# One routing search prepared in two parts instead of four, and low parts of probabilities moved from VectorE to GpSimd in heads 23 to 29

## The chip, the cores and the metric

The kernel runs on one core of a Trainium2 chip. The metric is the device time of one execution in microseconds. Three timed runs of the kernel before gave 721.38, 722.83 and 725.23 us, median 722.83 us; the profiled execution took 720.61 us.

## The reference

Attention in 4 batches of 8 heads, 768 queries and keys, 64 channels; a query sees only the keys of its own hash bucket. Then a mixture of 8 experts, in which every token goes to one expert and every expert takes 384 tokens, filled in the order of the logits.

```python
q_bits = (np.einsum('bhsd,dk->bhsk', q, proj) > 0)
...
scores = np.where(mask, scale * np.matmul(q, k.transpose(0, 1, 3, 2)), -1e9)
attn = np.exp(scores - np.max(scores, axis=-1, keepdims=True))
attn = attn / (np.sum(attn, axis=-1, keepdims=True) + 1e-09)
x = np.matmul(attn, v)            # then (3072 tokens, 512)
logits = x @ w_gate
for idx in np.argsort(-logits.flatten()):
    tok, e = (int(idx) // E, int(idx) % E)
    if assigned[tok] >= 0 or counts[e] >= cap: continue
    assigned[tok] = e; counts[e] += 1
out[mask] = np.maximum(x[mask] @ w1[e], 0.0) @ w2[e]
```

## The kernel before

**Steps.** Attention goes through 32 heads (head 8b+j belongs to batch b), and each head through 6 steps, one for each chunk of 128 keys; heads 30 and 31 end it. The order of all instructions is written out by hand: `ORD='SF0r1LRA'` says in which order a step issues its parts, and a dictionary `at` holds other work by half step (step t has the half steps 2t, issued at `r`, and 2t+1, issued at `R`), so that 12 half steps are one head. A number n in the change is such a half step: 326 lies in head 27.

**The parts of a step.** `S` is a pass for the row maximum of a later head, nine steps ahead: TensorE makes 768 masked scores for 128 queries into `pss` (L250), which has two buffers, and VectorE reduces them to one column (L252). `0` and `1` make the scores of one chunk of keys in halves of 384 queries (L281, L282) and ScalarE takes the exponential into `pt` (L283). `L` makes the low part of the last step's probabilities: `lo` is `pt` in float32 less its own upper 16 bits (L287 for one chunk, L290 for two at once). Which engine does it is a table: for each head a list of chunks that VectorE takes (a number 10+i means chunks 2i and 2i+1 in one instruction); GpSimd takes the rest. `A` multiplies four steps later the high and low parts with the values (L304 to L306), and after a head's last chunk a small product subtracts what the maximum's row added (L310, L311). VectorE then divides (`norm`, L318 to L322, into `X`).

**Between heads.** Once a head's six reductions are done, TensorE transposes the maxima into a buffer of `pss` (`m_rows`, L261) and ScalarE writes them to a row of `qa` (L262). TensorE takes its instructions in order, so a pass or an `m_rows` whose reduction is late holds all behind it. After each second head ScalarE copies the quotients to float16 (`xhigh`, L330), VectorE subtracts (`xlow`, L332), and a DMA transposes the result; after a batch's last head the logits of the batch are made on TensorE (L361, L362) and summed by VectorE (L363).

**The early search.** The first expert's search needs for each of 24 columns of tokens (6 for each batch) the best expert, a sort key and its first digit. `early` gives ten VectorE instructions for a range of columns: L568 to L573, L581, L577, L578 and the comparison with 128 thresholds, L586. Before the change it is called once for each batch, and its instructions are spread five half steps apart, from half steps 268, 300 and 332 for the first three batches; those of the last batch run after attention, when TensorE has only the search to do. GpSimd also makes, for each group of four heads, four low parts of queries and keys (L139).

```python
def lo(h,kc,eng,n=1):
    ...
    eng.tensor_tensor(l,p,p.bitcast(BF)[:,1::2],op=ALU.subtract)
```

Of the kernel before, what the change touches and what calls it, by code (L numbers as in the profile page):

```python
# [8 lines left out]
F32 = mybir.dt.float32  # L9
# [9 lines left out]
AP=dict(PAT=[[10], [5]],  # L19
 ORD='SF0r1LRA',  # L20
 LAG=4,
 VM=[2, 2, 2, 2],
 LL=[4, 3, 3, 2, 2, 2],
 EL={30: [10, 3, 4, 5], 31: [10, 11, 4, 5]},
 E0=[3, 5],
 E1=[],
 X=[4, 4, 18, 14],
 XE=0,
 MR=2,
 LEAD=9,  # L30
# [5 lines left out]
 P4=[-33, -33, -25, -21, -13, -7, -11, -7, -20, -16, -5, -2, -7, 5, 8, 3, 1, 4, 14, -56, -51, -11],  # L36
 CV=[3, 4, 5, 6],
 L0=[89, 4],
 EA=[268, 32, 5],
 MO=['', 'AKs', 'BqLk', 'lm', 'c|ABqKLslmk', 'ABqKLsklm|c', 'ABqKLsklm|c'],  # L40
 MD=[2, 9, 8],
 MV=[23, 24, 28, 57, 96, 1],
# [7 lines left out]
def attention(tc, nc, ctx, qT, kT, vv, proj, wg, x_dram, L, jp, identf, ident, B, late=None, after=None):  # L50
# [4 lines left out]
    psT=ctx.enter_context(tc.tile_pool(name="psT",bufs=NB["T"],space=PS))  # L55
    psV=ctx.enter_context(tc.tile_pool(name="psV",bufs=NB["V"],space=PS))
# [26 lines left out]
    wps=psV.tile([128,512],F32,name="psv")  # L83
# [208 lines left out]
    def AV(h,kc):  # L292
# [14 lines left out]
        if kc==5:  # L307
            for c in range(6):

                if j==3: T.matmul(av[:,c,:],QA[u][96:128,j,c*128:c*128+128],WF[u][96:128,j,:],start=False,stop=(c==5),skip_group_check=True,tile_position=(96,0))  # L310
                else: T.matmul(av[:,c,:],QA[u][:,j,c*128:c*128+128],WF[u][:,j,:],start=False,stop=(c==5),skip_group_check=True)  # L311
    X={}; XS={}; normed=set(); turned={}
    def norm(h):
        d=h//2
        if h%2==0: X[d]=dp.tile([128,6,128],F32,name="X")
        av=AVt[h][:,0:390].rearrange("p (c d) -> p c d",c=6)
        r=dp.tile([128,6],F32,name="r6")
        V.tensor_scalar(r,av[:,:,64],1e-9,1.0/SX,op0=ALU.add,op1=ALU.mult)  # L318
        V.reciprocal(r,r)
        normed.add(h)  # L320
        for c0,c1 in ((0,3),(3,6)) if h==NH-1 else ((0,6),):
            V.tensor_tensor(X[d][:,c0:c1,h%2*64:h%2*64+64],av[:,c0:c1,0:64],r[:,c0:c1,None].to_broadcast([128,c1-c0,64]),op=ALU.mult)  # L322
    XT6=XT.rearrange("p d c q -> p (d c q)").bitcast(F16).rearrange("p (d c z q) -> p d c z q",d=4,c=6,z=2)
# [3 lines left out]
    def xhigh(g):  # L327
        need(g,0,1)
        XS[g]=dp.tile([128,6,2,128],F16,name="XS")
        A.copy(XS[g][:,:,0],X[g])  # L330
    def xlow(g,eng):
        eng.tensor_tensor(XS[g][:,:,1],X[g],XS[g][:,:,0],op=ALU.subtract)  # L332
        xout(g,True)
    def xpart(g,x,c0=0,c1=6):
        need(g,x)
        if x==0: XS[g]=dp.tile([128,6,2,128],F16,name="XS")
        r=slice(64*x,64*x+64)
        A.copy(XS[g][:,c0:c1,0,r],X[g][:,c0:c1,r])
        V.tensor_tensor(XS[g][:,c0:c1,1,r],X[g][:,c0:c1,r],XS[g][:,c0:c1,0,r],op=ALU.subtract)
    def xout(g,turn):  # L340
        b,d=divmod(g,4)
        if turn: turned[d]=b; SY.dma_start_transpose(XT6[:,d].rearrange("p c z q -> p (c z) q"),XS[g].rearrange("p c z q -> p (c z q)"))
        SY.dma_start(x_dram[b*768:(b+1)*768,256*d:256*d+256].rearrange("(c p) e -> p c e",p=128),XS[g].rearrange("p c z q -> p c (z q)"))
# [23 lines left out]
    def add(n,f,*a):  # L367
        if n>=2*(6*NH+LAG+6): raise ValueError('an operation has no step')
        at.setdefault(n,[]).append((f,a))
# [8 lines left out]
    n=-1; early=[]  # L378
# [6 lines left out]
    for G in range(1,NG):  # L385
# [11 lines left out]
        for j in range(4):  # L397
            n=48*(G-1)+AP['CV'][j] if G>3 else p[15]+st*j
# [10 lines left out]
    for h in range(1,NH,2):  # L409
        b,d=h//8,h%8//2; n=2*(6*h+5+LAG)+AP['X'][0]  # L410
        if h==NH-1: n=2*(6*h+5+AP['LL'][5])
        if h==NH-1:
            for c in (0,3): add(n,xpart,4*b+d,1,c,c+3)
            for hf in range(2): add(n+AP['X'][1]*hf,xtr,b,d,hf)
            add(n+4,logits,b,[d]); add(n-5,xpart,4*b+d,0)
            add(n,xout,4*b+d,False)
        else:
            add(n,xhigh,4*b+d); add(n+AP['X'][1],xlow,4*b+d,(V,G_)[AP['XE']])
        if h==NH-1: pass
        elif b==B-1: add(n+AP['X'][3],logits,b,[d])  # L420
        elif d==3: add(n+AP['X'][2],logits,b,range(4))
        if after and d==3:
            for i,f in enumerate(after(b,lambda: psT.tile([128,512],F32,name="pst"),lambda: psV.tile([128,512],F32,name="psv"))):
                add(n+5 if b==B-1 else max(n+AP['X'][2]+3,AP['EA'][0]+AP['EA'][1]*b)+AP['EA'][2]*i,f)
    for n,f in enumerate(late or ()): add(AP['L0'][0]+AP['L0'][1]*n,f)
    for n in sorted(x for x in at if x<0):
# [10 lines left out]
    def step(o,t):  # L437
# [8 lines left out]
        elif o=='L' and t>=1 and (t-1)//6<NH:  # L446
            hh,ss=divmod(t-1,6)
            on=AP['E0'] if hh<1 else AP['E1'] if hh<2 else AP['EL'].get(hh,AP['PAT'][hh%len(AP['PAT'])])
            if 10+ss//2 in on:
# [38 lines left out]
class Moe:  # L488
    def __init__(s, tc, nc, ctx, N):
        s.tc,s.nc,s.N=tc,nc,N  # L490
        s.NC=NC=N//128; s.CAP=N//8
        s.cp=ctx.enter_context(tc.tile_pool(name="mcp",bufs=1)); s.zp=ctx.enter_context(tc.tile_pool(name="mzp",bufs=2))
        s.IDX={}; s.XG={}; s.W={}; s.WIX={}; s.late=[]; s.pend=[]; s.gate=None

    def consts(s):

        nc,NC,cp=s.nc,s.NC,s.cp; G_=nc.gpsimd; A=nc.scalar
        todo=[]
        def iota(shape,pat,cm=0,base=0,name=None,dt=F32):
            t=cp.tile(shape,dt,name=name)  # L500
            todo.append(lambda: G_.iota(t,pattern=pat,base=base,channel_multiplier=cm,allow_small_or_imprecise_dtypes=True))
            return t
        def fill(shape,v,name,dt=F32):
            t=cp.tile(shape,dt,name=name)
            todo.append(lambda: G_.memset(t,v)); return t
# [4 lines left out]
        todo.append(lambda: G_.tensor_tensor(s.ntri,s.ntri,ntd,op=ALU.add))  # L510
        s.ones=fill([128,128],1.0,"mones",BF); s.one48=fill([128,2*NC],1.0,"one48")
        col=lambda v,n,dt=BF: fill([128,1],v,n,dt).to_broadcast([128,128])
# [18 lines left out]

        s.gp=cp.tile([128,2,2,NC],BF,name="gp")
        for i,v in enumerate((1.0,-1.0)):
            todo.append(lambda i=i,v=v: A.activation(s.gp[:,i,0,:],iof[:,0:NC],AF.Copy,scale=128.0*v))
            todo.append(lambda i=i,v=v: A.activation(s.gp[:,i,1,:],pcol.to_broadcast([128,NC]),AF.Copy,scale=v))
        s.th=iota([128,4,NC],[[128,4],[0,NC]],0,4097,name="th")
# [72 lines left out]

    def z(s,shape,dt,name,**k): return s.zp.tile(shape,dt,name="z"+name,**k)  # L610

    def early(s,b,ps,wps,nb=4):

        NC=s.NC; n=NC//nb; c0=b*n
        if b==0:
            s.Z={k:s.z(sh,dt,k,bufs=1) for k,sh,dt in (
                ("m",[128,NC],F32),("eq",[128,NC,8],F32),("mx",[128,NC],F32),("mxu",[128,NC],BF),("OH",[128,NC,8],BF),
                ("key",[128,NC],I32),("D",[128,6,NC],I32),("E",[128,6,NC],BF))}
            s.Z["cmp"]=[s.z([128,NC//2,32 if i else NT[0],2],BF,f"cmp{i}",bufs=1) for i in range(3)]
        todo=s.best(s.Z,c0,c0+n,True)  # L620
        todo.append(lambda: s.compare(s.Z["cmp"][0],0,s.Z["E"][:,0],c0,c0+n))
        if b==nb-1:
            def rest():
                s.ps0=ps; s.wps=wps; s.ph0=s.phase(0)
                for _ in range(7): next(s.ph0)
            todo.append(rest)
        return todo
# [318 lines left out]
@with_exitstack  # L946
def tile_bucket_attention_moe(ctx, tc, qT, kT, vv, proj, wg, w1, w2, out):
    nc = tc.nc
    B = qT.shape[0] // 2
    drp = ctx.enter_context(tc.tile_pool(name="drp", bufs=1, space=DR))  # L950
    x_dram = drp.tile([768 * B, 1024], F16, name="x_dram")
    M = Moe(tc, nc, ctx, 768 * B)
    late = M.consts()
    with ExitStack() as c1:
        c1.enter_context(tc.manual_schedule())
        attention(tc, nc, c1, qT, kT, vv, proj, wg, x_dram, M.Lm, M.jp, M.identf, M.ident, B, late, M.early)
    with ExitStack() as c2:
        M.open(c2, x_dram, w1, w2, out)
        with tc.manual_schedule():
            M.start()  # L960
            M.run()
# [34 lines left out]
```

## Time and profile before

| what | value |
|---|---|
| median of three timed runs | 722.83 us |
| the profiled execution's own time | 720.61 us |
| its span | 718.8 us |
| TensorE (PE) busy | 662.8 us, 92% |
| VectorE (DVE) busy | 545.0 us, 76% |
| GpSimd (POOL) busy | 527.8 us, 73% |
| ScalarE (ACT) busy | 391.4 us, 54% |

The shares are means over stages that differ. In the 40 slices of the page, of 18 us each, attention fills the first 21 or so; TensorE's granted clock is at full speed there, falls where the first search runs, and is back for the experts. The page's table of groups names the costliest instructions; its chain of waits ends at the last DMA and says nothing of attention. For this change the stretch to look at is the last third of attention.

### The profile page before, as it was taken

Reading aid. Unit: us, or ns where it says so; the run is one execution under the profiler, and the core shown is the slowest. Engines: PE = TensorE matmul, PEld = TensorE weight load, DVE = VectorE, ACT = ScalarE, POOL = GpSimd, SP = SyncE. Lnnn points to the kernel's source line nnn. Section 1 sums busy time; section 2 is a strip of 40 time slices with the busy share of each in tenths; the row PEclk is TensorE's granted clock in tenths of the full one; section 3 lists DMA queues with packets and bytes.
Section 4 is the critical chain, followed back from the end, with each engine's and each line's share of the span. In section 5 each row is a group of like instructions: output and inputs, shape, how many; then the busy total and the mean of one; then the engine's idle time right before and its main releaser. Section 6 shows DMA issues by size and latency. Waiting matters only on the chain. (4 is left out here: it accounts for less than half of the span.)

```text
span 718.8 us, 19139 instructions
## 1 busy us (share of the span) xinstructions
PE 662.8 (92%) x7874; PEld 429.9 (60%) x7889; DVE 545.0 (76%) x1231; ACT 391.4 (54%) x772; POOL 527.8 (73%) x463
## 2 busy tenths in 40 slices
PE   8899998999999999889897679989899999999995
PEld 2466675777767776667675465555555555555552
DVE  6888887889899898999878755787788787834120
ACT  5767775867777777656562142434444444444530
POOL 7598979988888988767630365777778787887851
PEclk8899999999999999999998568999999999999998
DMA  8539858826778376542012352626181717272601
GB/s 220 157 94 197 206 145 205 198 66 150 166 168 201 63 175 135 137 100 47 2 46 68 102 179 73 221 70 238 45 279 58 267 58 265 60 278 97 239 17 45
DMA packets 63520, 99.49 MB, mean 138 GB/s; under 512 B 28116, under 2 KB 54088, under 8 KB 61384
## 3 DMA queue, kind: packets, MB, share of 16 engines
q1 hardware_dynamic: 56568, 52.11, 30.5%
q0 software_dynamic: 6784, 46.14, 18.3%
q8 instruction: 62, 1.02, 0.6%
q14 instruction: 26, 0.21, 0.1%
q10 hardware_dynamic: 80, 0.00, 0.0%
HBM read 59.53 MB, written 12.58 MB: 100 GB/s over the span
## 5 line engine op out<-in xcount | busy, mean ns | idle before, releaser
L287 POOL TENSOR_TENSOR lo<-pt 128x768 f16<-128x768 f32 x137 | 230.5, 1699 | 50.4 <-ACT pt L283 46.8
L283 ACT ACTIVATE pt<-pst 128x384 f32<-128x384 f32 x384 | 171.1, 491 | 94.8 <-PE pst L282 91.9
L252 DVE TENSOR_REDUCE m<-pss 128x1 f16<-128x770 f32 x192 | 180.6, 955 | 32.6 <-PE pss L250 32.0
L306 PE MATMUL psv<-vh,lo 128*128 128x65 f16 x1152 | 124.1, 194 | 3.1 <-POOL lo L287 3.1
L281 PE MATMUL pst<-qa,ka 128*128 128x384 f16 x384 | 125.3, 327 | 1.6 <-ACT qa L267 0.8
L282 PE MATMUL pst<-qb,kb 128*128 128x384 f16 x384 | 125.3, 327 | 1.0 <-DMA qb<-ql 1.0
L304 PE MATMUL psv<-vh,pt 128*128 128x65 f16 x1152 | 124.7, 194 | 0.2 <-DVE X L322 0.2
L305 PE MATMUL psv<-vl,pt 128*128 128x64 f16 x1152 | 124.7, 193 | 0.0
L304 PEld LDWEIGHTS <-pt 128*128 128x128 bf16 x1152 | 107.1, 98 | 17.0 <-issue 3.1
L305 PEld LDWEIGHTS <-pt 128*128 128x128 bf16 x1152 | 105.9, 98 | 10.3
L306 PEld LDWEIGHTS <-lo 128*128 128x128 f16 x1152 | 105.9, 97 | 3.9 <-POOL lo L287 3.7
L250 PE MATMUL pss<-ka,qa 128*128 128x385 f16 x384 | 95.5, 331 | 11.7 <-DVE m L252 8.1
L852 PE MATMUL ph<-xx,wh 128*128 128x384 f16 (+1 forms) x544 | 102.6, 323 | 2.8 <-DVE hl L855 2.8
L829 POOL TENSOR_TENSOR wl<-wf,wh 128x512 bf16<-128x512 f32 x87 | 98.5, 1151 | 0.1
L817 ACT CAST wh<-wf 128x1024 f16<-128x1024 f32 x64 | 65.6, 1043 | 31.1 <-DVE un L757 21.0
L854 ACT ACTIVATE hh<-ph 128x384 f16<-128x384 f32 x64 | 31.4, 490 | 82.2 <-PE ph L852 82.2
L852 PEld LDWEIGHTS <-wh 128*128 128x128 f16 x544 | 51.4, 100 | 34.7 <-issue 5.3
L855 DVE SCALAR_TENSOR_TENSOR hl<-ph,hh 128x384 f16<-128x384 f32 x64 | 34.7, 553 | 34.4 <-ACT hh L854 33.8
L864 PEld LDWEIGHTS <-hh 128*128 128x128 f16 x384 | 34.9, 97 | 34.4
L852 PE MATMUL ph<-xx,wl 128*128 128x384 f16 (+1 forms) x272 | 54.8, 322 | 0.0
L282 PEld LDWEIGHTS <-kb 128*128 128x128 f16 x384 | 37.4, 97 | 23.6 <-issue 3.4
L281 PEld LDWEIGHTS <-ka 128*128 128x128 f16 x384 | 37.6, 98 | 22.8 <-issue 2.3
(266 smaller groups left out, 1198.3 us busy)
## 6 DMA issues: line engine op xcount, KB each, us to landing
vp<-in_vv_dram SPq DMA_DIRECT2D x8, 768.0 KB
x_dram<-XS SPq DMA_DIRECT2D x16, 384.0 KB
qp<-in_qT_dram SPq DMA_DIRECT2D x7, 768.0 KB
kp<-in_kT_dram SPq DMA_DIRECT2D x7, 768.0 KB
qa<-qh SPq DMA_DIRECT2D x14, 192.0 KB
ka<-kh SPq DMA_DIRECT2D x14, 192.0 KB
qb<-qh SPq DMA_DIRECT2D x14, 192.0 KB
kb<-kh SPq DMA_DIRECT2D x14, 192.0 KB
```

Of the source, the lines that this page charges most:

```text
L250: T.matmul(ps[:,hf,0:HK],QA[u][:,j,qc*128:qc*128+128],KA[u][:,j,hf*HK:hf*HK+HK],start=True,stop=True)
L252: V.tensor_reduce(M6[h][:,qc:qc+1],ps[:,:,0:HK],axis=AX.XY,op=ALU.max,negate=True)
L281: T.matmul(ps[:,0:384],KA[u][:,j,kr],QA[u][:,j,r],start=True,stop=False)
L282: T.matmul(ps[:,0:384],KB[u][:,j,kr],QB[u][:,j,r],start=False,stop=True)
L283: A.activation(PT[h,kc][0][:,r],ps[:,0:384],AF.Exp,scale=0.125)
L287: eng.tensor_tensor(l,p,p.bitcast(BF)[:,1::2],op=ALU.subtract)
L304: T.matmul(av[:,c,:],ph[:,r],VH[u][:,j,kc,:],start=(kc==0 and c==0),stop=False,skip_group_check=True)
L305: T.matmul(av[:,c,0:64],ph[:,r],VL[u][:,j,kc,:],start=False,stop=False,skip_group_check=True)
L306: T.matmul(av[:,c,:],l[:,r],VH[u][:,j,kc,:],start=False,stop=False,skip_group_check=True)
L817: s.nc.scalar.copy(h[:,r],f[:,r])
L829: for _ in range(n): s.nc.gpsimd.tensor_tensor(*s.pend.pop(0)[1],op=ALU.subtract)
L852: T.matmul(p[:,r],a[:,o:o+128],b[:,d,r],start=n==0 and not c,stop=n==11 and c in (None,2),skip_group_check=c is not None)
```

## The change

The table `EL` gets lists of its own for heads 23 to 29. Before, even heads had [10] there and odd heads [5], 10 chunks together on VectorE; now 6, and GpSimd makes 4 more. The early search of the first three batches is called once, for 18 columns, in place of three times for 6, with its first instruction at half step 326. The copy to float16 comes half a step later after each pair of heads. The logits of the first three batches come one and a half steps later, and those of the first three pairs of heads of the last batch one step later.

```diff
- EL={30: [10, 3, 4, 5], 31: [10, 11, 4, 5]},
+ EL={23: [], 24: [10], 25: [11], 26: [], 27: [3], 28: [3], 29: [], 30: [10, 3, 4, 5], 31: [10, 11, 4, 5]},
- X=[4, 4, 18, 14],
+ X=[5, 4, 20, 15],
- EA=[268, 32, 5],
+ EA=[262, 32, 5],
+ EG={2: 0, 3: 3},
...
-        if after and d==3:
-            for i,f in enumerate(after(b,...
+        if after and d==3 and b in AP['EG']:
+            for i,f in enumerate(after(AP['EG'][b],b,...
                 add(n+5 if b==B-1 else max(n+AP['X'][2]+3,AP['EA'][0]+AP['EA'][1]*b)+AP['EA'][2]*i,f)
...
-    def early(s,b,ps,wps,nb=4):
-        NC=s.NC; n=NC//nb; c0=b*n
-        if b==0:
+    def early(s,a,b,ps,wps,nb=4):
+        NC=s.NC; c0=a*NC//nb; c1=(b+1)*NC//nb
+        if a==0:
...
-        todo=s.best(s.Z,c0,c0+n,True)
+        todo=s.best(s.Z,c0,c1,True)
```

On VectorE, before the quotients of head 23 (the rows L318 belong to them; `m` are maxima, `lo` low parts, `zeq`, `zkey`, `zmxu` the early search), the order before was:

```order
L571 TENSOR_TENSOR zeq<-zeq,wt 128x48
L252 TENSOR_REDUCE m_5975<-pss 128x1 x3
L572 TENSOR_TENSOR zkey<-zm,zkey 128x6
L287 TENSOR_TENSOR lo<-pt 128x768
L252 TENSOR_REDUCE m_5975<-pss 128x1 x2
L290 TENSOR_TENSOR lo<-pt 128x1536
L573 TENSOR_REDUCE zmxu<-zeq 128x6
L252 TENSOR_REDUCE m_6215<-pss 128x1
L318 TENSOR_SCALAR r_6244<-psv 128x6
```

At the same place the changed kernel has (its line numbers are one higher):

```order
L253 TENSOR_REDUCE m_5972<-pss 128x1 x5
L291 TENSOR_TENSOR lo<-pt 128x1536
L253 TENSOR_REDUCE m_6209<-pss 128x1
L319 TENSOR_SCALAR r_6238<-psv 128x6
L320 RECIPROCAL r_6238<-r_6238 128x6
L323 TENSOR_TENSOR X<-psv,r_6238 128x6x64
```

The single low part and three instructions of the early search are gone; the pair of low parts stays. Between the quotients of heads 27 and 28, VectorE had before:

```order
L570 TENSOR_SCALAR zkey<-zm 128x6
L252 TENSOR_REDUCE m_7171<-pss 128x1
L586 TENSOR_TENSOR zcmp_370<-zE,tb_93 128x768
L252 TENSOR_REDUCE m_7171<-pss 128x1
L571 TENSOR_TENSOR zeq<-zeq,wt 128x48
L252 TENSOR_REDUCE m_7171<-pss 128x1 x2
L332 TENSOR_TENSOR XS<-X,XS 128x6x128
L252 TENSOR_REDUCE m_7171<-pss 128x1
L572 TENSOR_TENSOR zkey<-zm,zkey 128x6
L252 TENSOR_REDUCE m_7392<-pss 128x1
L318 TENSOR_SCALAR r_7422<-psv 128x6
```

and has now:

```order
L253 TENSOR_REDUCE m_7155<-pss 128x1
L288 TENSOR_TENSOR lo<-pt 128x768
L253 TENSOR_REDUCE m_7155<-pss 128x1
L573 TENSOR_TENSOR zkey<-zm,zkey 128x18
L253 TENSOR_REDUCE m_7155<-pss 128x1 x2
L574 TENSOR_REDUCE zmxu<-zeq 128x18
L333 TENSOR_TENSOR XS<-X,XS 128x6x128
L253 TENSOR_REDUCE m_7155<-pss 128x1
L253 TENSOR_REDUCE m_7374<-pss 128x1
L319 TENSOR_SCALAR r_7404<-psv 128x6
```

Four instructions of the early search became two, and head 28's low part of chunk 3 stands here in place of a pair one head boundary earlier. On TensorE at attention's end, the last two logits of the third pair of heads of the last batch (L362, from `XT`) stood before the products of the last head's last chunk (L304):

```order
L362 LDWEIGHTS XT
L362 MATMUL pss<-wgs,XT 128x8
L304 LDWEIGHTS pt
L304 MATMUL psv<-vh_209,pt 128x65
L305 LDWEIGHTS pt
L305 MATMUL psv<-vl_210,pt 128x64
```

Now these logits (L362 and L363 with the new numbers) follow those products and their last correction (L311):

```order
L311 LDWEIGHTS qa_171
L311 MATMUL psv<-wf_212,qa_171 128x65
L362 LDWEIGHTS XT
L362 MATMUL pss<-wgs,XT 128x16
L362 LDWEIGHTS XT
L362 MATMUL pss<-wgs,XT 128x16
```

They moved behind everything that the last head's quotients wait for, and stand in front of the transposes of these quotients. GpSimd's list has 33 low parts where it had 29 after its last low part of keys, with nothing else moved.

## Rows read from the trace of the kernel before

**Rows 1.** Busy time by stretch: us, PE, PEld, DVE, ACT, POOL, clock, DMA.

```profile
200.00:290.00 90.00, 88.69 (x1407) 64.48 (x1399) 79.36 (x102) 65.32 (x146) 78.61 (x58) 1.00 0.67 153
290.00:374.00 84.00, 75.83 (x1208) 56.15 (x1207) 77.21 (x107) 51.11 (x104) 53.78 (x33) 1.00 0.28 65
```

**Rows 2.** The same view of four shorter stretches.

```profile
298.00:304.00 6.00, 3.65 (x56) 2.57 (x53) 5.93 (x9) 3.72 (x8) 2.44 (x2) 1.00 0.47 108
312.00:318.00 6.00, 3.94 (x68) 2.82 (x65) 5.90 (x9) 2.76 (x7) 2.71 (x3) 1.00 0.61 116
336.00:350.00 14.00, 12.23 (x192) 8.80 (x189) 12.84 (x22) 7.54 (x15) 7.97 (x5) 1.00 0.25 59
350.00:364.00 14.00, 12.09 (x182) 8.74 (x182) 10.93 (x15) 8.72 (x18) 10.84 (x7) 1.00 0.24 58
```

**Rows 3.** Waits of PE from 290 to 374: us in total, times, longest.

```profile
PE pss L250 <- DVE m L252: 3.6, 6, 2.0
PE pss L261 <- DVE m L252: 2.8, 2, 1.9
```

**Rows 4.** Timeline at the first two gaps: start, duration, instruction, [idle before].

```profile
295.52 2.29 DVE L287 TENSOR_TENSOR lo<-pt 128x768 f16<-128x768 f32 x1
299.47 2.70 DVE L290 TENSOR_TENSOR lo<-pt 128x1536 f16<-128x1536 f32 x1
303.20 0.49 PE L250 MATMUL pss<-ka,qa 128*128 128x385 f16 x2 [2.05 <-DVE m L252]
313.12 1.42 DVE L577 TENSOR_TENSOR zE<-zD,sc 128x6 bf16<-128x6 int32 x1
```

**Rows 5.** Timeline, PE at an earlier boundary of heads.

```profile
279.48 0.49 PE L250 MATMUL pss<-ka,qa 128*128 128x385 f16 x2 [0.46 <-DVE m L252]
```

**Rows 6.** DVE groups from 255 to 389.2, early search: busy us, mean ns.

```profile
L577 DVE TENSOR_TENSOR zE<-zD,sc 128x6 bf16<-128x6 int32 x3 | 3.4, 1119 | 0.0
...
L573 DVE TENSOR_REDUCE zmxu<-zeq 128x6 bf16<-128x48 f32 x3 | 0.6, 189 | 0.0
```

**Rows 7.** Timeline, DVE: first and last early instruction of the last batch.

```profile
389.30 0.20 DVE L568 TENSOR_REDUCE zm<-Lm 128x6 f32<-128x48 f32 x1
...
390.54 0.56 DVE L586 TENSOR_TENSOR zcmp<-zE,tb 128x768 bf16<-128x768 bf16 x1
```

**Rows 8.** Groups by form: the comparison of 24 columns in later searches.

```profile
L586 DVE TENSOR_TENSOR zcmp<-zE,tb 128x3072 bf16<-128x3072 bf16 x5 | 8.8, 1753 | 0.0
```

**Rows 9.** Timeline, DVE: a pair and a single of low parts.

```profile
346.06 1.75 DVE L290 TENSOR_TENSOR lo<-pt 128x1536 f16<-128x1536 f32 x1
...
366.77 0.95 DVE L287 TENSOR_TENSOR lo<-pt 128x768 f16<-128x768 f32 x1
```

**Rows 10.** GpSimd's low parts from 290 to 374, as a group.

```profile
L287 POOL TENSOR_TENSOR lo<-pt 128x768 f16<-128x768 f32 x31 | 51.3, 1672 | 29.4 <-ACT pt L283 29.3
```

**Rows 11.** Timeline, GpSimd: head 23's chunk 4, and the longest low part.

```profile
295.53 1.46 POOL L287 TENSOR_TENSOR lo<-pt 128x768 f16<-128x768 f32 x1
...
346.47 2.67 POOL L287 TENSOR_TENSOR lo<-pt 128x768 f16<-128x768 f32 x1 [4.73 <-ACT pt L283]
```

**Rows 12.** Timeline, PE: the correction that ends head 23.

```profile
299.71 0.35 PE L310 MATMUL psv<-wf,qa 32*128 32x65 f16 x6
```

**Rows 13.** Timeline, DVE: quotients of heads 25 and 26.

```profile
327.85 0.56 DVE L322 TENSOR_TENSOR X<-psv,r 128x384 f32<-128x384 f32 x1
...
337.72 0.56 DVE L322 TENSOR_TENSOR X<-psv,r 128x384 f32<-128x384 f32 x1
```

**Rows 14.** Timeline, PE at attention's end.

```profile
383.71 0.30 PE L361 MATMUL pss<-wgs,XT 128*128 128x16 f16 x6
...
386.57 0.87 PE L351 MATMUL pst<-identf,X 128*128 128x128 f32 x6 [0.88 <-DVE X L322]
```

**Rows 15.** ScalarE groups from 0 to 390: exponentials and copies of quotients.

```profile
L283 ACT ACTIVATE pt<-pst 128x384 f32<-128x384 f32 x384 | 171.1, 491 | 94.8 <-PE pst L282 91.9 <-POOL ql L139 1.3 <-POOL lo L287 0.2
...
L330 ACT CAST XS<-X 128x768 f16<-128x768 f32 x15 | 12.5, 832 | 0.3
```

More of the change, by code (lines that the diff above doesn't have):

```diff
@@ L421, in attention @@
         elif d==3: add(n+AP['X'][2],logits,b,range(4))
-        if after and d==3:
-            for i,f in enumerate(after(b,lambda: psT.tile([128,512],F32,name="pst"),lambda: psV.tile([128,512],F32,name="psv"))):
+        if after and d==3 and b in AP['EG']:
+            for i,f in enumerate(after(AP['EG'][b],b,lambda: psT.tile([128,512],F32,name="pst"),lambda: psV.tile([128,512],F32,name="psv"))):
                 add(n+5 if b==B-1 else max(n+AP['X'][2]+3,AP['EA'][0]+AP['EA'][1]*b)+AP['EA'][2]*i,f)
@@ L619, in early @@
             s.Z["cmp"]=[s.z([128,NC//2,32 if i else NT[0],2],BF,f"cmp{i}",bufs=1) for i in range(3)]
-        todo=s.best(s.Z,c0,c0+n,True)
-        todo.append(lambda: s.compare(s.Z["cmp"][0],0,s.Z["E"][:,0],c0,c0+n))
+        todo=s.best(s.Z,c0,c1,True)
+        todo.append(lambda: s.compare(s.Z["cmp"][0],0,s.Z["E"][:,0],c0,c1))
         if b==nb-1:
```

## The prediction

> **What bounds the kernel now.** I read the page's slices first: TensorE is the engine nearest to full in attention, and from slice 17 on it is less full than before although its clock stays up. The view of busy time by stretch puts numbers on that [rows 1]. From 200 to 290 us PE is busy 88.69 of 90 us, so it sets the pace; 1.31 us are lost. From 290 to 374 it is busy 75.83 of 84, so 8.17 us are lost, while VectorE is busy 77.21 of 84 and GpSimd only 53.78. The clock is 1.00 in both. Four shorter stretches [rows 2] hold nearly all of the loss: 6.00 - 3.65 = 2.35 us at 298 to 304, 2.06 at 312 to 318, 1.77 at 336 to 350 and 1.91 at 350 to 364, together 8.09. In the first two VectorE is full (5.93 and 5.90 of 6). The waits name the cause [rows 3]: PE waits for row maxima, 3.6 us in front of a pass and 2.8 us in front of the transposes of a head's maxima. The reductions themselves are not slow; the timeline shows what stands in front of them [rows 4]: a low part of 2.29 and a pair of 2.70 us, then a pass of PE that has waited 2.05; later a six-column product of the early search that takes 1.42 us.
>
> So in this third of attention VectorE's list sets the end, at the boundaries of heads, and what it is spared can be worth up to 8.1 us. All that follows attention starts from its end, so what is won there moves the end of the kernel by as much.
>
> **The early search.** Before, the first three batches take thirty VectorE instructions, in ten groups of three that run from 3.4 us down to 0.6 [rows 6], 16.3 us in all. The same ten instructions for the last batch run when GpSimd has nothing, and there they take from 0.20 (the first) to 0.56 us (the comparison), 2.2 us for the ten [rows 7]. Thirty without disturbance would be 6.6 us; 9.7 us are therefore stretching, 0.32 us for each. The ten new ones have three times the columns. The comparison lies between 0.56 us for 6 columns [rows 7] and 1.75 for 24 [rows 8]; on the straight line 18 columns cost 1.35. The other nine are near their fixed cost at 6 columns; I give five of them (48 elements to 144) 0.12 us more each, an estimate that is small beside the rest. Alone: 2.2 + 0.8 + 0.6 = 3.6 us. With the same stretching for each, 10 x 0.32, the sum is 6.8. VectorE is spared 16.3 - 6.8 = 9.5 us, nothing of it in the last batch, whose ten are the same.
>
> **What stretches them.** The product L577 takes 1119 ns on average over the three batches [rows 6] while the whole of the last batch's ten takes 2.2; the reduction L573 keeps its 189 ns. GpSimd's low parts are stretched too: 1672 ns on average, 1.46 for an undisturbed one, 2.67 for the longest, which starts beside a pair on VectorE [rows 9 to 11]. The Trainium skill (SBUF — State Buffer, Who interferes with whom) says that a VectorE instruction with two SBUF inputs and a GpSimd instruction that reads SBUF exclude each other for the whole instruction, while a reduction is never held. The trace agrees, with L577 and L573. By that rule the stretching is paid for each instruction whatever its columns, so that a third of the instructions pays a third; if it grew with the columns instead, the ten would cost 9.7 + 3.6 = 13.3 and only 3.0 be spared. The rule also speaks against the change: four more low parts on GpSimd keep the port longer. That is the second rival.
>
> **The low parts.** VectorE loses the singles of heads 23, 25, 27 and 29 and the pairs of heads 26 and 28, and gets a pair in 25 and singles in 27 and 28. With 2.29 for head 23's [rows 4], 1.75 for a pair and 0.95 for a single [rows 9]: 2.29 + 3 x 0.95 + 2 x 1.75 - 1.75 - 2 x 0.95 = 5.0 us spared. GpSimd gets four more, 4 x 1.67 = 6.7 us [rows 10], beside 29.4 us that it idles there for want of exponentials. Two places are tight. Head 23: GpSimd ends chunk 4 at 295.53 + 1.46 = 296.99 [rows 11], chunk 5 would end at 298.45, and the products that need it end at 299.71, where the correction starts [rows 12], so they begin about half a us earlier, at 299.2. It is in time by 0.7 us, less what PE wins before; I charge 0.3, bounds 0 and one whole call, 1.5. Heads 26 to 29 have 22 low parts on GpSimd (6, 5, 5, 6); a head at PE's pace is 337.72 - 327.85 = 9.87 us [rows 13], four are 39.5, and 22 x 1.67 = 36.7. That fits, and the products come four steps after the scores, so a late call is first paid from that.
>
> **What it is worth on the path.** VectorE is spared 9.5 + 5.0 = 14.5 us of 77; it then stands at 63 of some 76 to 78 us, 82%, below the 79.36 of 90 (88%) of the earlier stretch, where PE loses 1.31 in 90. But not each gap closes. Gap by gap, with the 0.46 us that PE waited at 279.48 behind a pair [rows 5] as the price of a boundary that still has something beside its reductions:
> - 298 to 304: the 2.29 single and three search instructions go, the pair stays. 2.35 - 0.46 = 1.9 won.
> - 312 to 318: the 1.42 product and a comparison with the row's maximum go, the subtraction of quotients stays. 2.06 - 0.46 = 1.6 won.
> - 336 to 350: the pair at the boundary goes, a single and four larger search instructions are spread over the stretch. I keep 0.5: 1.3 won.
> - 350 to 364: two search instructions remain of four, a single is added away from the boundary. Two boundaries, I keep 0.8: 1.1 won.
>
> Together 5.9. What is late next is PE itself, at 9.87 us a head.
>
> **The moved copies and logits.** A copy (0.83 us) goes behind one more exponential (0.49 us) [rows 15]; ScalarE waits 91.9 us for PE's scores in attention, which hides it. It moves the subtraction behind it by less than a step. I take nothing, bounds -1.0 and +1.0, two exponentials to either side. At the end, the logits of the last batch's third pair stood before the products that the last quotients wait for; they run for about 0.30 us [rows 14], and now they run while PE waits 0.88 us for the quotients. 0.3 won, bounds 0 and 0.3. The larger comparison (+0.8) and one-hot stand in front of head 30's chunk 5 on VectorE, whose products come three steps later, some 4 us: nothing, and up to 0.8 if that cover is gone. SP's queue gets one load in front of a transpose: nothing.
>
> **Sum.** 5.9 + 0.3 - 0.3 = 5.9 us. The profiled execution took 720.61 (span 718.8); it becomes 714.7. It lies 2.2 below the median of the runs, 722.83; against that the forecast is **716.9 us**. Its own bounds: all gaps closed, the end's 0.3 and 1.0 from the copies, 9.4 won, 713.4; nothing won from 336 on (1.9 + 1.6 + 0.3), less 1.5 for head 23, 2.3 won, 720.5.
>
> **Rivals.**
> - *The last heads stay bound by VectorE.* From half step 326 on the search issues an instruction every five half steps, as one batch alone did before, and these are larger. Then the 3.7 us of gaps after 336 stay, and 1.9 + 1.6 + 0.3 - 0.3 = 3.5 is won: 719.3. For it: 12.84 of 14 us busy at 336 to 350. Against: 10.93 of 14 at 350 to 364, where VectorE often waits for PE, and the pairs are gone.
> - *The port takes the saving.* With GpSimd busy nearly all the time in heads 26 to 29, each of the eight new instructions other than the two reductions waits for a whole low part, 8 x 1.46 = 11.7; with 3.6 alone they cost 15.3 against 16.3. Then only 6.0 of 14.5 us are spared, and 5.9 x 6.0/14.5 = 2.4 is won: 720.4. For it: L577 was held for 1.4 at 313.12. Against: the mean hold was 0.32, in a stretch with GpSimd at 64%.
> - *GpSimd becomes the bound (slower).* If its 22 low parts in heads 26 to 29 took the longest row's 2.67 us, they would need 58.7 us against 39.5; the three steps by which a call may lag pay 4.6, and PE waits 14.6, more than the 5.9 won: 731.5. It decides from a mean of (39.5 + 4.6 + 5.9) / 22 = 2.27 us on. Against: the mean is 1.67, and the fewer VectorE low parts hold it less.
>
> **Chances.** Forecast 0.68, first rival 0.17, second 0.10, slower 0.05. A measurement of this kernel can tell about 0.5%, 3.6 us, from no change. The forecast and half of the first rival lie beyond it, less a little for a forecast that falls short: faster 0.73. Same 0.22, slower 0.05. The range that leaves two in ten outside goes from 713.5 to 721.3: it holds the forecast's own 713.4 to 720.5 nearly whole, and the first two rivals.
>
> **What would show it.** In the changed kernel's trace PE should lose about 2 us in the same heads in place of 8.2, with waits for maxima of 1 to 3 us in place of 6.4. Attention's end, the last batch's first early instruction (389.30 before), should come near 383.4, and what follows should take as long as before. The early search should be ten instructions of 6 to 8 us together; over 12 speaks for the port. GpSimd's mean low part in heads 26 to 29 should stay under 1.8 us, and no product should wait for a low part by more than 1 us in all; waits of several us there would show the third rival. The forecast is wrong if PE's waits go and the span does not, or if new waits for ScalarE's rows of maxima take their place.

## The result and the profile after

The changed kernel takes **714.15 us** (median of 4 runs, 711.66 to 716.35) beside 723.52 for the kernel before (4 runs, 721.38 to 725.23): a ratio of 0.9871, 95% interval 0.9824 to 0.9918. By the bound of half a per cent it is faster, by 9.4 us where 5.9 were forecast; six more executions of it (e4 below) give 0.9892, 7.8 us. Ratios here and below leave out the few executions more than 1.5% above the fastest of their kernel. The profiled execution took 711.66, its span is 709.9.

Busy time by stretch, after (columns as in [rows 1]; attention now ends about 7 us earlier, so the second stretch is cut at 368):

```profile
200.00:290.00 90.00, 87.99 (x1376) 64.07 (x1373) 79.77 (x101) 66.26 (x145) 78.56 (x58) 1.00 0.67 154
290.00:368.00 78.00, 75.28 (x1232) 56.43 (x1230) 63.55 (x86) 51.71 (x107) 58.21 (x36) 1.00 0.29 66
```

In the last third of attention PE now loses 78 - 75.28 = 2.72 us in place of 8.17, and VectorE is busy 81% of the stretch in place of 92%. What PE still waits for there, in the view of PE's waits from 285 to 370:

```profile
PE pss L251 <- ACT qa L263: 1.7, 2, 0.9
PE pss L251 <- DVE m L253: 0.6, 2, 0.4
PE pss L262 <- DVE m L253: 0.3, 1, 0.3
```

The waits for maxima are 0.9 us, against 6.4 in [rows 3]. The first line, PE waiting for ScalarE's rows of maxima, is not new; the same view of before, from 290 to 374, has it too:

```profile
PE pss L250 <- ACT qa L262: 1.5, 2, 0.8
```

It is now what is left.

The timeline of VectorE after: the pair at the boundary that used to wait beside a single, three of the ten instructions of the prepared search, its comparison, and the first instruction of the last batch's search.

```profile
296.68 1.83 DVE L291 TENSOR_TENSOR lo<-pt 128x1536 f16<-128x1536 f32 x1
...
327.90 0.29 DVE L569 TENSOR_REDUCE zm<-Lm 128x18 f32<-128x144 f32 x1
...
336.05 0.95 DVE L571 TENSOR_SCALAR zkey<-zm 128x18 int32<-128x18 int32 x1
...
346.01 0.57 DVE L573 TENSOR_TENSOR zkey<-zm,zkey 128x18 int32<-128x18 int32 x1
...
367.53 1.35 DVE L587 TENSOR_TENSOR zcmp<-zE,tb 128x2304 bf16<-128x2304 bf16 x1
...
381.68 0.20 DVE L569 TENSOR_REDUCE zm<-Lm 128x6 f32<-128x48 f32 x1
```

The ten together take 0.29 + 0.31 + 0.95 + 0.59 + 0.57 + 0.29 + 0.63 + 0.40 + 0.68 + 1.35 = 6.06 us (forecast 6.8), the comparison exactly the 1.35 of the straight line. The last row answers to 389.30 in [rows 7]: 7.6 us earlier (forecast 5.9), of which 4.2 belong to the start of the kernel, as the table of stages below shows.

GpSimd's low parts from 318 to 368, as a group (busy, mean ns, idle before):

```profile
L288 POOL TENSOR_TENSOR lo<-pt 128x768 f16<-128x768 f32 x23 | 35.7, 1577 | 12.5 <-ACT pt L284 7.7 <-issue 3.7 <-DVE Lm L364 0.9
```

Their mean fell from 1672 [rows 10] to 1577 ns although there are more of them, and among PE's waits from 285 to 370 none is for a low part.

Set against the kernel before by stage (from the division of one head to that of another, L322 before and L323 after), the two spans of 718.8 and 709.9 differ so:

| stage | before | after | won |
|---|---|---|---|
| start to head 0 | 41.67 | 37.48 | 4.2 |
| heads 0 to 9 | 107.21 | 107.97 | -0.8 |
| heads 9 to 20 | 120.57 | 122.46 | -1.9 |
| heads 20 to 22 | 21.36 | 21.37 | 0.0 |
| heads 22 to 31 | 95.35 | 89.23 | **6.1** |
| after head 31 | 332.64 | 331.39 | 1.3 |

The stage that the prediction spoke of won 6.1 us against 5.9. The 4.2 at the start is nothing of the change: neither the search nor the last heads' low parts run there. In the same view of stretches, PE at 15 to 20 us, before and then after:

```profile
15.00:20.00 5.00, 4.19 (x16) 1.55 (x13) 2.15 (x3) 1.62 (x3) 2.28 (x2) 0.50 0.53 103
```

```profile
15.00:20.00 5.00, 3.75 (x25) 2.14 (x24) 4.00 (x5) 3.42 (x7) 2.55 (x2) 1.00 0.56 109
```

The clock column says 0.50 in one execution and 1.00 in the other: half speed, the 1.2 of 1.2 and 2.4 GHz. Over the fourteen traces of this study head 0 ends between 37.4 and 42.2 us, and the stage after head 31 takes 330.3 to 334.3. Differences there belong to the single execution.

The second profile of the kernel before (e5) gives 95.31 us for heads 22 to 31, beside 95.35, and the traces after (three with all parts in: after, e4, e7) give 89.23, 89.22 and 89.21. That the two of before agree to 0.04 us is partly chance. Heads 22 to 23 take 12.67 us in the first and 10.78 in e5, heads 23 to 25 take 24.37 and 26.22, and in e5 a stretch at reduced clock lies among the latter (0.71 over 320 to 324). After and e4 agree head by head within 0.01 us. Heads 20 to 31 together take 116.7 us in the first trace of before, 120.8 in e5, and 110.6 in each of the three after: 6.1 or 10.2 us won, by the trace of before that is taken.

### The profile page after: what moved, and what is told of

It reads as the page before. It is cut to its first block, busy times and chain, and to the rows that moved or that the text cites. A ratio compares the mean times of both kernels' runs of the same rounds, so it can differ in the third digit from the quotient of the medians.

```text
span 709.9 us, 19131 instructions
## 1 busy us (share of the span) xinstructions
PE 657.6 (93%) x7889; PEld 428.0 (60%) x7889; DVE 532.3 (75%) x1208; ACT 392.6 (55%) x772; POOL 535.4 (75%) x467
## 5 line engine op out<-in xcount | busy, mean ns | idle before, releaser
L288 POOL TENSOR_TENSOR lo<-pt 128x768 f16<-128x768 f32 x141 | 235.9, 1691 | 38.8 <-ACT pt L284 33.2
L251 PE MATMUL pss<-ka,qa 128*128 128x385 f16 x384 | 94.3, 327 | 10.6 <-DVE m L253 6.9
```

What stands on the lines that cost most here:

```text
L251: T.matmul(ps[:,hf,0:HK],QA[u][:,j,qc*128:qc*128+128],KA[u][:,j,hf*HK:hf*HK+HK],start=True,stop=True)
```

## The experiments

Three parts can be taken one by one: **low** (the table EL), **search** (EG, EA and early's two arguments) and **copies** (the table X). I ran all eight combinations. Each ratio is against executions of the kernel before taken beside it, in three sets with the medians in the first row. Won is (1 - ratio) x 722 us, uncertain by 2 to 3 us by the intervals; the last two columns are stages of each run's one profile.

| kernel | median us | ratio, 95% | won | heads 20-22 | heads 22-31 |
|---|---|---|---|---|---|
| before | 721.90, 722.49, 722.54 | | | 21.36 | 95.35 |
| e5: before again | 724.94 | 1.0036 [1.0002, 1.007] | -2.6 | 25.47 | 95.31 |
| e1: low | 721.52 | 0.9994 [0.9962, 1.0025] | 0.4 | 23.90 | 92.63 |
| e2: search | 721.14 | 0.9995 [0.9966, 1.0024] | 0.4 | 25.34 | 94.57 |
| e3: copies | 719.79 | 0.9969 [0.9936, 1.0003] | 2.2 | 22.89 | 91.66 |
| e6: low, search | 716.65 | 0.9915 [0.9881, 0.9949] | 6.1 | 23.82 | 90.09 |
| e9: low, copies | 718.55 | 0.9936 [0.9901, 0.997] | 4.6 | 22.89 | 91.06 |
| e10: search, copies | 719.16 | 0.996 [0.9927, 0.9993] | 2.9 | 21.35 | 92.85 |
| e4: all three again | 713.19 | 0.9892 [0.9853, 0.993] | 7.8 | 21.35 | 89.22 |
| e8: all, search in threes | 718.65 | 0.9926 [0.9887, 0.9966] | 5.3 | 21.35 | 93.25 |
| e7: all, no VectorE low parts | 714.51 | 0.992 [0.988, 0.9959] | 5.8 | 21.36 | 89.21 |
| e11: low, search, pair moved | 716.61 | 0.9924 [0.9894, 0.9953] | 5.5 | 21.97 | 90.09 |
| e12: e11, copies late from head 23 | 714.31 | 0.9913 [0.9879, 0.9947] | 6.3 | 21.98 | 88.96 |

e5 sets the measure: the same kernel against itself came out 2.6 us apart, so a difference of that size between two lines of whole times decides nothing by itself.

**e1, low alone.**

```diff
- EL={30: [10, 3, 4, 5], 31: [10, 11, 4, 5]},
+ EL={23: [], 24: [10], 25: [11], 26: [], 27: [3], 28: [3], 29: [], 30: [10, 3, 4, 5], 31: [10, 11, 4, 5]},
```

> The low parts alone: the new lists for heads 23 to 29, search and copies as before. Theory (VectorE's list sets the pace in heads 23 to 29, and what it is spared is won in proportion): 5.0 of the 14.5 us that the whole change spares VectorE, so a third of the 6.1 us that the changed kernel's trace won between the quotients of head 22 and the end of attention, about 2 us: ratio 0.997. Rival (the gaps come from two lows and a pair standing together, the search is beside the point): 298 to 304 and the boundary at 349 close, 3.5 to 4.5 us, ratio 0.994. Rival (more low parts on GpSimd stretch the search that stays): nothing won, ratio 1.000 or above, with the thirty search instructions over 17 us.

Nothing measurable in whole times: 0.4 us. In the trace its heads 22 to 31 are 2.7 us shorter, its heads 20 to 22 2.5 longer than in the first trace of before. The thirty search instructions take 16.3 us as before, so they are not stretched more. A late maximum has come up at another place: a comparison of the old search, which takes 0.56 us alone [rows 7], takes 1.82, and PE waits behind it:

```profile
352.63 1.82 DVE L586 TENSOR_TENSOR zcmp<-zE,tb 128x768 bf16<-128x768 bf16 x1
...
355.38 0.49 PE L250 MATMUL pss<-ka,qa 128*128 128x385 f16 x2 [1.79 <-DVE m L252]
```

**e2, search alone.** The diff of EA, EG and early as in the change, EL and X as before.

```diff
- EA=[268, 32, 5],
+ EA=[262, 32, 5],
+ EG={2: 0, 3: 3},
```

> The search alone: one call for three batches from half step 326, low parts and copies as before. Theory in proportion: 9.5 of 14.5 us spared, so about 4 us won of 6.1, ratio 0.9945; ten search instructions of 5 to 7 us together. Rival (low parts are what matters): 1 to 2 us won, ratio 0.998. Rival (what stretches an instruction grows with its columns): ten instructions of some 13 us, 1.5 us won.

Again 0.4. The ten instructions take 5.7 us together, so VectorE is spared 10.6, and still the last stage takes 94.57. The first two boundaries nearly close, although the single of head 23 and the pairs are back: heads 22 to 24 take 21.79 us, in the first trace of before 26.04. What is lost is lost later. Before the quotients of head 27 a pair of low parts and a prepared instruction of the search, lengthened to 1.57 us, stand one behind the other:

```profile
343.11 1.75 DVE L291 TENSOR_TENSOR lo<-pt 128x1536 f16<-128x1536 f32 x1
344.78 1.57 DVE L572 TENSOR_TENSOR zeq<-zeq,wt 128x144 f32<-128x144 f32 x1
...
347.27 0.49 PE L262 MATMUL pss<-ident,m 128*128 128x128 f16 x6 [2.27 <-DVE m L253]
```

Heads 26 to 28 take 26.29 us, before 23.25. In the changed kernel that pair is gone and the instruction takes 0.59 us. PE's waits in e2 from 262 to 362:

```profile
PE pss L251 <- DVE m L253: 3.9, 4, 2.2
PE pss L262 <- DVE m L253: 2.6, 2, 2.3
```

and two stretches of e2 behind the longest two, of 2.20 and 2.27 us, in which the clock was granted at half for a while:

```profile
278.00:284.00 6.00, 4.89 (x50) 3.23 (x50) 3.71 (x7) 2.26 (x5) 4.57 (x3) 0.72 0.00 0
348.00:356.00 8.00, 7.28 (x66) 4.68 (x65) 2.89 (x5) 4.35 (x8) 3.89 (x3) 0.58 0.00 0
```

**e3, copies alone.**

```diff
- X=[4, 4, 18, 14],
+ X=[5, 4, 20, 15],
```

> The later copies to float16 and later logits alone. The prediction gave them nothing but 0.3 us at attention's end, bounds -1.0 and +1.0: ratio 0.9985 to 1.001. Rival (the part of the measured 9.4 us that the last heads do not explain, about 3 us, comes from this edit, which is the only one that touches heads 0 to 22): ratio 0.996, with head 22's quotients 2 to 4 us earlier than before while the clock at the start is the same.

It won the most of the three, where I had put nothing: 2.2 us in whole times (the interval just reaches no change), 3.7 in heads 22 to 31 of the trace. The quotients of head 22 did not come earlier, as the rival had it: 295.1 us, before 290.8. Its VectorE rows at the boundary that cost 2.06 us in [rows 2] show how:

```profile
315.01 0.45 DVE L577 TENSOR_TENSOR zE<-zD,sc 128x6 bf16<-128x6 int32 x1
315.38 0.94 DVE L332 TENSOR_TENSOR XS<-X,XS 128x768 f16<-128x768 f32 x1
```

Before, the subtraction of quotients stood first, and what followed it is the 1.42 of [rows 4]:

```profile
311.66 1.54 DVE L332 TENSOR_TENSOR XS<-X,XS 128x768 f16<-128x768 f32 x1
...
315.59 0.49 PE L261 MATMUL pss<-ident,m 128*128 128x128 f16 x6 [1.89 <-DVE m L252]
```

A copy half a step later puts the subtraction later too; there it is not held (0.94 for 1.54), nor is the product ahead of it (0.45 for 1.42), and PE's wait for the transposes of the maxima falls from 1.89 to 0.78 us.

**e4, all three again**, the changed kernel beside e1 to e3.

> The changed kernel once more. Two of its first four runs took 712 and two 716 us, and in its profiled run TensorE's granted clock stayed at 1.00 between 10 and 25 us where before it had 0.68, 0.50 and 0.80, and the first head ended 4.2 us earlier. Theory (that is chance of the start, not the change): the ratio comes out nearer to one than 0.987, at 0.990 to 0.992 (6 to 7 us), and the profile wins 6 us between the quotients of head 22 and attention's end whatever its start did. Rival (the edits win about 9 us): ratio 0.987 again.

7.8 us. The sum of the three alone is 3.0; with 2 to 3 us of uncertainty on each they hardly add, and the traces of e1 and e2 show why: what is left of the old load meets something else at the next boundary.

**e6, e9 and e10, two parts at a time.** The diffs are those above, two at a time.

> The low parts and the search together, copies and logits at their old places. Alone the low parts won 0.4 us, the search 0.4, the copies 2.2 (each +-2.3), all three 7.8. Theory (a gap at a head's boundary has two causes, a low part and search instructions, and stays wide while either is there; the copies only shift it): the two together win most of it, 6 to 8 us, ratio 0.989 to 0.992, mean granted clock near 0.970. Rival (the copies' new place is the third condition, since they decide what the subtraction behind them meets): 2 to 4 us, ratio 0.995 to 0.997.

> The low parts and the copies, with the search batch by batch as before. Theory (the search stays in the boundaries of heads 23 to 28, so the gaps do): the sum of the two alone, 2 to 3 us, ratio 0.996 to 0.997. Rival (every two of the three edits give most): 0.991 to 0.993.

> The search and the copies, with the low parts shared as before. Theory (the single and the pairs stay at the boundaries): the sum of the two alone, 2 to 3 us, ratio 0.996 to 0.997. Rival (every two of the three edits give most): 0.991 to 0.993. In its profile a boundary gap of over 2 us should be followed by a stretch at the lower granted clock, as after 278 and 346 us in the run with the search alone.

With these the eight corners are there. Copies win 2.2 alone, 4.6 - 0.4 = 4.2 beside low, 2.5 beside search, 1.7 beside both: four times the same sign, about 2.6. Low wins 0.4 alone and 2.4 beside copies, but 5.7 beside search and 4.9 beside both. Search wins 0.4 alone and 0.7 beside copies, but 5.7 beside low and 3.2 beside both. So low and search need each other, and copies stand nearly by themselves. Each of these differences is uncertain by some 3 us: the common signs count, not the size of any one. In heads 22 to 31 of the traces the picture is milder, since low alone already wins 2.7 us there. And e9, at 0.9936, lies between its two expectations.

**e8, the change with each of the ten search instructions cut into three of six columns again**, issued one behind the other at the same ten places.

```diff
-        todo=s.best(s.Z,c0,c1,True)
-        todo.append(lambda: s.compare(s.Z["cmp"][0],0,s.Z["E"][:,0],c0,c1))
+        def one(k0,k1): return s.best(s.Z,k0,k1,True)+[lambda: s.compare(s.Z["cmp"][0],0,s.Z["E"][:,0],k0,k1)]
+        todo=[lambda fs=fs: [f() for f in fs] for fs in zip(*(one(6*k,6*k+6) for k in range(a,b+1)))]
```

> The changed kernel with each of the ten search instructions of the first three batches issued as three of six columns, one behind the other at the same place: thirty instructions, everything else as changed. Theory (an instruction pays its fixed cost and one hold whatever its columns): 20 more at about 0.22 alone and 0.1 to 0.3 of holding, less 1.4 for the columns, so 5 to 9 us more of VectorE in heads 27 to 30, and 2 to 4 us of the gain lost: ratio 0.992 to 0.995. Rival (what the merge saves is hidden; only the low parts and the place matter): ratio 0.989 as the changed kernel.

It gives back 2.5 us of whole time and 4.0 of heads 22 to 31. Three of its groups, whose counterparts after take 0.95, 0.57 and 0.63 us:

```profile
342.80 2.37 DVE L571 TENSOR_SCALAR zkey<-zm 128x6 int32<-128x6 int32 x3
...
354.11 1.99 DVE L573 TENSOR_TENSOR zkey<-zm,zkey 128x6 int32<-128x6 int32 x3
...
365.16 2.06 DVE L582 TENSOR_SCALAR zD<-zkey 128x6 int32<-128x6 int32 x3
```

The thirty take 10.73 us against 6.06 for the same columns, and PE's waits for maxima (290 to 375) are back:

```profile
PE pss L251 <- DVE m L253: 4.0, 5, 1.2
...
PE pss L262 <- DVE m L253: 0.3, 1, 0.3
```

The same columns cost more in more instructions, but not three times as much. Each of the three groups shown takes 1.42 or 1.43 us more than its counterpart, about one low part of GpSimd (1.46 in [rows 11]), together 4.27 of the 4.67 us of excess; the other seven groups pay 0.4 between them. The 2.5 us of whole time are within the uncertainty, the 4.0 of the stage are not: the three traces of the change agree there within 0.02.

**e5, the kernel before again**, to see what of its first trace repeats.

> The kernel before, once more, for a second trace of it. Theory (the gap that the runs with the low parts alone, the search alone and both without the copies have at head 21's boundary, 1.5 to 2.2 us behind a single and a pair that GpSimd holds up, is chance and falls on before too, though its first trace does not show it): from the quotients of head 20 to those of head 22 it takes 23 to 25 us in place of 21.4, or a boundary gap of over 2 us elsewhere is followed by a stretch at half clock. Rival (the edits themselves cause it): 21.4 us again. From head 22 to head 31 both expect 92 to 96 us, against 89.2 in the changed kernel's two traces. Ratio 1.000.

Heads 22 to 31 repeat in sum (95.31), heads 20 to 22 do not: 25.47 against 21.36. The pair at the end of head 21, VectorE first and then GpSimd, in the first trace of before:

```profile
276.80 1.75 DVE L290 TENSOR_TENSOR lo<-pt 128x1536 f16<-128x1536 f32 x1
...
277.21 2.66 POOL L287 TENSOR_TENSOR lo<-pt 128x768 f16<-128x768 f32 x1 [1.12 <-ACT pt L283]
```

and in e5, where GpSimd was ahead, with PE's wait behind it:

```profile
280.58 2.72 DVE L290 TENSOR_TENSOR lo<-pt 128x1536 f16<-128x1536 f32 x1
...
280.21 1.47 POOL L287 TENSOR_TENSOR lo<-pt 128x768 f16<-128x768 f32 x1 [2.22 <-ACT pt L283]
281.64 3.15 POOL L139 TENSOR_TENSOR kl<-kp,kh 128x768 f16<-128x768 f32 x1
...
284.22 0.80 PE L250 MATMUL pss<-ka,qa 128*128 128x385 f16 x2 [2.20 <-DVE m L252]
```

Who starts first, by 0.4 us, goes with 0.46 us of waiting [rows 5] or 2.20. Of the five profiles with the copies as they were and the pair in its place (before, e5, e1, e2, e6) the last four have GpSimd first and the wait of 2.20; in all seven with the copies moved (e3, e4, e7 to e10, after) VectorE is first and the wait is not there. In after:

```profile
275.32 1.75 DVE L291 TENSOR_TENSOR lo<-pt 128x1536 f16<-128x1536 f32 x1
...
275.85 2.55 POOL L288 TENSOR_TENSOR lo<-pt 128x768 f16<-128x768 f32 x1 [1.13 <-ACT pt L284]
```

**e7, six more low parts on GpSimd**: no low part of heads 23 to 29 on VectorE.

```diff
- EL={23: [], 24: [10], 25: [11], 26: [], 27: [3], 28: [3], 29: [], 30: [10, 3, 4, 5], 31: [10, 11, 4, 5]},
+ EL={23: [], 24: [], 25: [], 26: [], 27: [], 28: [], 29: [], 30: [10, 3, 4, 5], 31: [10, 11, 4, 5]},
```

> The changed kernel with all low parts of heads 23 to 29 on GpSimd: six more calls there, six less of chunks on VectorE. Theory (GpSimd has room until its calls in a head need more than PE's 9.9 us): 42 calls at 1.6 to 1.7 us are 67 to 71 us against 69 to 75 us of the seven heads, so PE begins to wait for low parts, 1 to 4 us; ratio 0.990 to 0.995. Rival (VectorE's pairs still cost more than GpSimd's room): up to 1 us better than changed, 0.988. Rival of the prediction (calls stretched to 2.3 us and more): 96 us for 42, slower than the kernel before.

```profile
290.00:368.00 78.00, 75.37 (x1230) 56.31 (x1227) 59.40 (x82) 51.44 (x107) 64.16 (x42) 1.00 0.28 65
```

GpSimd is busy 64.16 us where it was 58.21, and PE as much as after (75.37 for 75.28). The stage takes 89.21. GpSimd has room for these low parts, and the 1 to 4 us of waiting that the theory gave are not there; the whole time is not distinguishable from the change.

**e11 and e12, looking for a better version.** e11 is e6 with head 22's pair taken at later chunks ([11] for [10], which runs at 281.95 us, behind the division of head 21); e12 is e11 with X's new values from head 23 on only.

```diff
- EL={23: [], 24: [10], 25: [11], 26: [], 27: [3], 28: [3], 29: [], 30: [10, 3, 4, 5], 31: [10, 11, 4, 5]},
+ EL={22: [11], 23: [], 24: [10], 25: [11], 26: [], 27: [3], 28: [3], 29: [], 30: [10, 3, 4, 5], 31: [10, 11, 4, 5]},
...
-        b,d=h//8,h%8//2; n=2*(6*h+5+LAG)+AP['X'][0]
+        b,d=h//8,h%8//2; X_=AP['X'] if h>=23 else [4,4,18,14]; n=2*(6*h+5+LAG)+X_[0]
```

> Low parts and search without the copies, and head 22's pair made of chunks 2 and 3 in place of 0 and 1, which moves it two steps away from the boundary of head 21. Theory (that pair, held beside GpSimd's low part of the keys, is what makes the runs without the copies slower on average than their best): heads 20 to 22 take 21.0 to 21.8 us, heads 9 to 20 stay at 120.6, ratio 0.988 to 0.990, better than the 0.9915 without it. Rival (the copies win by something else): ratio 0.9915 again.

> The whole change with head 22's pair moved as in the run beside it, and with the later copies and logits only from head 23 on. Theory (in heads 9 to 20 the later copies cost 1.8 to 2.8 us in every trace that has them, 122.4 to 123.4 against 120.6, and from head 22 on they win 0.9): heads 9 to 20 at 120.6, 22 to 31 at 89.2, ratio 0.985 to 0.988, better than the changed kernel. Rival (the copies' 2.2 us are won in the early heads): ratio 0.990 to 0.992.

The long form is gone from heads 20 to 22 in both (21.97, 21.98), yet e11 is no faster than e6 in whole time, though heads 20 to 31 of its trace are 1.9 us shorter (112.06 for 113.91). A difference of that size is within the uncertainty, so what the collision alone is worth stays open. e12 has the shortest heads 22 to 31 of all, 88.96, but its ratio lies where its rival put it, and neither beats the change.

## Why the prediction was right, and which term was off

- **What bounds the stage: right.** VectorE's list at the boundaries of heads did. With 10.3 us of search and 5.8 us of low parts less on it (forecast 9.5 and 5.0), PE's waits for maxima fell from 6.4 to 0.9 us, and the stage became 6.1 us shorter; the sum of the four gaps was 5.9.
- **The four gaps: right in sum, in part by luck.** Heads 22 to 23 won 2.2 us (the first gap, forecast 1.9), heads 23 to 24 1.8 (1.6), heads 26 to 27 1.3 (1.3), but heads 27 to 28 only 0.2 of 1.1. The last gap was misread: of the 1.91 us lost at 350 to 364, 1.5 were PE's two waits for ScalarE's rows of maxima, which the change does not touch and which are 1.7 after. Heads 24 to 26, which had no term, won 0.8 and made up for it.
- **The search: right in count and size**, 6.06 us for 6.8. The reason given, that a hold is paid for each instruction, holds in part: in e8 thirty instructions pay a second hold at three places of ten, and cost 1.8 times the ten, not three times.
- **GpSimd as the bound: refuted**, by the mean of 1577 ns and by e7. The 0.3 charged for head 23 was not paid: PE waits for no low part there. The two rivals that left 3.5 or 2.4 us of gain fall with the 6.1 us of the stage.
- **The moved copies: put at nothing, for a reason that looked at the wrong engine.** I put 0 with bounds of 1.0 to either side and argued with ScalarE, which has time to spare. The four differences in whole times have one sign and a mean of 2.6 us, outside the bounds; but each is uncertain by some 3 us, and the kernel before differed from itself by as much as that mean, so the sign is likely and the size stays open. What I did not follow is the order on VectorE: the subtraction that goes with the copy changes its place against the search and against GpSimd, and is held less there. In e3 that nearly closes the second gap. In the changed kernel it shows before the quotients of head 25: the subtraction takes 2.02 us in e6, which is the change without the copies, and 1.13 in after (lines below). In heads 22 to 31 that is worth 0.9 us (90.09 in e6, 89.22 in e4), within the bounds; in heads 20 to 22, where VectorE's pair comes first with the copies moved, 2.5 (23.82 and 21.35). Without the copies the rest wins 6.1 us in whole times (e6); with them 7.8 to 9.4.
- **A sum of spared time would have been wrong.** 5.0 us for the low parts and 9.5 for the search, priced in proportion, would give them 2 and 4 us each alone. They won 0.4 each, and 6.1 together. The boundary at 303, where a single, search instructions and a pair stood in one row [rows 2, 4], closed with either (and in e5 with neither); but with low alone a comparison of the old search came in the way at 353, with search alone a pair beside a search instruction at 344.
- **The base was a good execution.** The first trace of before has the short form of heads 20 to 22, and most others without the moved copies don't. In e5 the gap at 303 is small and the one at the end of head 21 large instead. I forecast from the median of runs, but took no term for what its trace hid. That the whole time won 9.4 or 7.8 us, and not the 6.1 of the stage, may come from there; the single profiles do not show how often each form occurs.

The subtraction before the quotients of head 25, in e6 and then in after:

```profile
329.03 2.02 DVE L333 TENSOR_TENSOR XS<-X,XS 128x768 f16<-128x768 f32 x1
```

```profile
328.11 1.13 DVE L333 TENSOR_TENSOR XS<-X,XS 128x768 f16<-128x768 f32 x1
```

The hold between the two engines is first what the rows of before and e5 show: whichever of VectorE's pair and GpSimd's low part started first kept its short time (1.75 or 1.47 us), and the other was lengthened (2.66 or 2.72). The Trainium skill (SBUF — State Buffer, Who interferes with whom) says the same, that the engine which issues first has the shared ports for its whole instruction and the other blocks. The two traces agree.

What the copies cost: they lengthen heads 9 to 20, in the traces by about 2.0 us (mean of six with them 123.0, of four without them 120.9; e5 and e8, which have a stretch at half clock there, and e11 and e12 are left out), and still win in whole times. One cause is the same in every trace. A scaling of a tile of signs takes 0.39 us in before; in after, beside a low part of GpSimd, it takes 1.59, and PE then waits:

```profile
155.12 1.59 DVE L159 TENSOR_SCALAR bt<-bt 128x768 f16<-128x768 f16 x1
...
157.92 0.49 PE L251 MATMUL pss<-ka,qa 128*128 128x385 f16 x2 [1.16 <-DVE m L253]
```

In the seven traces with the copies moved there it takes 1.14 to 1.61 us and heads 9 to 10 take 12.73 to 12.80; in the seven others it takes 0.38 to 0.39, and the heads 11.31 to 11.32.

What stays open: which share of the copies' gain comes from heads 20 to 22, which from later heads, and which from fewer stretches at half clock was not separated. Forcing the order of the pair and GpSimd's low part at the end of head 21 was not tried.

## What to carry to other kernels

When an engine's list is late only at certain places, price a change by those places and by what else stands in the row there: one of two causes taken away may be worth next to nothing, because what is left meets something else at the next boundary, and both together most of it. An instruction that moves by half a step on one engine drags its followers on the others; list what they come to stand beside there before it is put down as nothing. And profile the kernel before twice, and compare head by head: a stage that differs between the two traces is not a base to count from, and a sum that agrees to 0.04 us can hide heads that differ by 1.9.

## What was not expected of the hardware

- Small VectorE instructions with one SBUF input are held too, not only those with two: in e8 three TENSOR_SCALAR of six int32 columns took 2.37 and 2.06 us in the last heads; in the last batch, where GpSimd has no low parts, one takes 0.16.
- From 100 us to the end of attention, a single wait of PE of some 2 us was followed by a stretch at half clock in e2 (2.20 and 2.27 us), e5 (2.08, 2.20 and 2.05), e8 (1.96) and e10 (2.26, then 0.57 over 346 to 350, as its expectation had it), but not behind the 2.05 us of [rows 4], nor behind 2.20 us in e1 and in e6. What decides between them is not shown.
- The time of the kernel before varies by itself from 716.97 to 729.39 us. Its 18 executions with a mean clock of 0.969 take 717.0 to 725.9 us, median 719.1, its three at 0.956 take 724.4 to 728.0: about 0.4 us for each 0.001, with a scatter as large as the effect. The mean over the runs was 0.964 for before and 0.971 for the change in e4, and 0.967 for the change in its first four runs.
